# A written-out task order for block-sparse attention followed by a max-out layer: one order replaced by another

## The chip, the core and the metric
The kernel runs on one core of one Trainium2 chip. The metric is the device time of one execution in microseconds (us); lower is better. The kernel before was run 11 times: median 173.11 us, lowest 172.62, highest 173.88.

## The reference, cut to what matters
Two layers. The first is attention with a local window and block summaries, for 4 batches, 8 heads, 768 positions and 64 channels. The second is a layer that takes the larger of two products and multiplies it by a third matrix.

```python
k_sum = k.reshape(B, H, nb, 32, D).max(axis=3)      # one summary key per 32 positions
v_sum = v.reshape(B, H, nb, 32, D).mean(axis=3)
scores_l = where(|i - j| < 16, scale * q @ k.T, -1e9)
scores_s = scale * q @ k_sum.T + log(32)
a = softmax(concat([scores_l, scores_s]))           # max, exp, sum, divide
x = a @ concat([v, v_sum])                          # then [B, H, S, D] -> [3072, 512]
out = maximum(x @ w1, x @ w2) @ w_out               # 512 -> 1024 -> 512, float32
```

## The kernel before, in words
**The work is cut into 679 tasks.** Each call of `op` (line 111) adds a task: an engine, or several that could do it, a function that emits its instructions, and the buffers that it reads and writes. Tasks are numbered in the order of these calls. Nothing is emitted until `Plan.run` (line 128) walks a string, `ORDER` (line 20). A word of it such as `P455:2` says: emit task 455 now, on engine P, and let the new buffer that it writes take slot 2 of its ring. P is TensorE (PE), A is ScalarE (ACT), D is VectorE (DVE), G is GpSimd (POOL), S is SyncE (SP), whose tasks are DMAs. So the string fixes three things: the order on each engine's queue, the engine of each task that has a choice, and the buffer slot. Each engine works through its own queue strictly in order, and semaphores hold it until the data of a task are there.

**The tasks**, with their numbers, as far as they are spoken of below. "b" is the batch, "hp" a pair of heads (0 to 3), "grp" one of three groups of 256 positions.

- *load k, load q* (line 298): 384 KB each from HBM to one of eight `land` slots; one pair per b and hp. For b = 0: k00 is 12, q00 13, k01 36, q01 37, k02 38, q02 39, k03 40, q03 41 (batch, then hp). k10 is 146, q10 147. *load v* (line 320): two of 768 KB per batch (14 and 16 for b = 0, 178 and 180 for b = 2).
- *cast k, cast q* to bf16, *turn* (transposes on PE, line 434), *place* (copy from PSUM), and for k also *max*, *wrap*, *sums* (summary keys): lines 425 to 467. turn k10 is 220 and turn q10 221; turn k22 is 323, its load 174, its cast 321.
- *scores* (line 469), *exp* on ACT (line 515), *mask* on DVE (line 509), *values* (PE, line 543), *inv* and *x* on DVE (lines 549 and 552), *turn x* (PE, line 575) and *xt* (its copy). xt 00 is made by tasks 120 and 125.
- *cast v, spread v, means* (PE, lines 346 and 349), *spread means*: v and its block means laid out in `vx` (lines 320 to 396). cast v21 is 181, means 20 is 188, spread means 1 is 169, spread means 2 is 193.
- *load w* (line 594): w1 and w2 in two halves, 1 MB each: 42 and 43 (first halves), 52 and 53 (second halves). From each half come two *wd* = w2 - w1 (44, 48, 54, 58) and two *w1b* (a bf16 copy of w1: 45, 49, 55, 59), then *turn w1* (PE, line 618: 46, 50, 56, 60) and *w1t* (its copy from PSUM: 47, 51, 57, 61).
- *load wo* (line 627): w_out in two halves of 1 MB (62 and 65), each cast into two *wo* (63, 64 and 66, 67).
- *w1o* (line 636) = w1 @ w_out, in four column blocks, each with two PE tasks of four 128x512 matmuls that add up in one PSUM bank: 446/447, 449/450, 452/453, 455/456 for blocks 0 to 3. The first of a pair needs w1t 0, 1 and wo 0, 1; the second w1t 2, 3 and wo 2, 3, and so the second halves of w1 and w_out. The copies of the results are 448, 451, 454, 457.
- *hidden* (line 660): eight 128x256 matmuls each, four tasks per b and grp, each with its own wd. 458, 460, 462, 464 are 000, 001, 002, 003 (b, grp, and which wd). *relu* is its copy from PSUM. *out* (lines 674 and 681): three tasks of four 128x512 matmuls for 128 rows, first x @ w1o, then twice relu @ wo; *copy out* and *store* follow.

max(x w1, x w2) w_out is computed as relu(x (w2 - w1)) w_out + x (w1 w_out), which is why w1o is needed.

**PE works in four array shapes**, as the operands have them: 128*128 (hidden, out, w1o, means of b = 0), 64 rows (turn, scores), 128*64 (values), 128*32 (means of later batches). A stretch in one shape is followed by a stretch in another, some 70 times in the kernel.

In the order before, SP loads k03, k01, k00, q02, q00, q01, k02, q03, v00, v01, w 42, w 43, wo 62, w 52, wo 65, w 53, and then batch 1 in the order q10, k10, q13, k12, k13, q11, q12, k11, v11, v10.

Of the kernel before, what the change touches and what calls it, by code (L numbers as in the profile page):

```python
# [17 lines left out]


ORDER = (  # L20
    "G5:0 D6:0 D1 D2 D0 S40:0,0 S36:1,0 S12:2,0 S39:3,0 G23:0,0,0 G4:0 S13:0 S37:0 A101:0 S38:0 G7 "
    "G32:0,0 P103:0,0 G8 S41:0 A105:1,0 G68:1 A77:2 S14:4 D106:0 G9 P70:2,0 G93:3 P79:4,0 S16:5 A72:2,0 "
    "D81:0,0 G10 P95:6,0 A69:0 S42:6 D108 D82:1 A78:1 P71:0 S43:7 D73:0 A76:0 P80:0 D3 D92:2 A85:1 D102:3 "
    "P94:0 A100:2 D83 P104:0 D107 D75 D84 A96:3,0 D74 S62:2 P90:2 D97:0 P86:4 A91:0 D15:0,0 A109:3 D98 "
    "P24:6 D18 D99 D19 P114:2 S52:1 A25 D21 A87:1 P88:0 D20 G22 P110:6 A89:2 P112:4 D17:0 S65:3 D26 A28 "
    "P33:0 D29 D27 A34 A113:3 D30 P116:0 D35 S53:0 A31 P126:4 A111:4 G45:0 D117:0 D127:1 D118:0,0 A49:1 "
    "D128:0 G48:0 P121:6 P46:0 D122:2 S147:4,0 D123:1,0 P50:4 A47:1,0 D51:0 P119:6 A120:0 P124:0 P136:4 "
    "D125 G63:0 A115:5 P131:6 P460:0 S146:0 D44:0 A64:0 D137:0 A461:0 P458:1 D138:0 G55:0 P455:2 A459 "
    "S153:5,0 D59:1 P56:3 P60:0 D57:0 P452:5 A61:0 D132:1 D67:0 P449:3 A66:0 D11:0 S150:2,0 D133:0 P446:4 "
    "P450 S152:0 P453 D58:0 S149:6,0 P456 A219:0 D54:0 S151:0 P447 A457:0 D218:1 S148:0 P129:0 P134:6 "  # L30
    "P462:2 G163:1,0,0,0 D130:1 A135 D454:0 S156:7 A448:0 P464:0 D463 A258:2 S154:3 P141:6 P221:4,0 "
    "A451:0 P220:0 P480:1 D257:3 A465 S171:0,0 D142:2 A222:0,0 P478:2 G231:0 D481:1 S173:1,0 P476:3 "
    "D226:0 A479 G246:1 P471:0 D223:1 P260:1,0 D224 P139:4 P259:0 D245:2 P472 A140:2 D143:0 G230:3 "
    "A261:2,0 S170:0 P482:4 D225 D265:1 A477 P484:5 A483 D262:0 P144:6 G157:0,0 P227:1 P247:3,0 A145 "
    "P248:0 P485 D249:1,0 A228:1 P232:6,0 S175:4,0 D263 P233:0 P473 A234:3,0 D229 S172:0 A253:2 P500:1 "
    "D251 D264 D236 D235:1 G155:0 A474:0 P486 A501:2 P496:2 A487:1 D237 S162 D238:3 G295:2 P164:3 S161 "
    "P494:4 G307:1 A165 D250:0 A168 A497 P489:0 G294:3 D166 A495 D167 P242:5 D158 S169 P239:1 P266:3 "
    "A243:2 P498:7 D159 A267:4 P490 D252 D244 P502:5 A499 D160 S178:5 A240:0 S180:2 P269:3 P254:6 D268 "
    "S174:0 P503 S196:6,0 D306:0 A270:3 P491 D241 A255:5 G187:0,0,0,0 P284:1 D271 P504 D285:0 A492:2 "
    "D286:2,0 P507:3 A505:3 S493 D256 P275:6 P272:0 P278:4 D276:1 P508 D273:2 G179:0,0 D279:0 D274:0,0 "  # L40
    "P466:2 D280:0 S177:7,0 D277:0 P287:0 P281:4 P467 D282:2 S195:3,0 D288:0 D283:0 P509 G181:0 D289:0 "
    "S199:0,0 P296:6,0 P297:0 D510:4 P290:4 S176:0 A298:0,0 P292:0 G322:3 D291:3 P468 A302:0 S186 G321:2 "
    "D293 P188:3 P308:4,0 G183 S198:0 P309:0 P324:6,0 A310:3,0 P323:0 D314:3 P518:0 S185 A329:1 D311:1 "
    "P514:1 A519:1 S182 P536:4 A469:5 S200:1,0 G382:0 A515 P512:5 S197:0 A325:2,0 P520:0 G333:1 A190 "
    "S194:0 D326:0 A189 P516:2 G334:3 A513 D313 P335:6,0 P336:0 D517 P530:1 A337:1,0 D537:2 A341:2 P521 "
    "D328 S184 D312 D327 D299:1 A371:2 P315:4 P330:6 P534:2 S201:0 A316:4 D339 D338:0 P522 S506 D192 D535 "
    "P532:4 A523:2 S470 D531 A331:0 P552:5 D300 D340 D301 P525:2 G383:1 D553:0 P303:0 D191 G370:3 P345:6 "
    "S193 P526 A304:1 D317 S202:5 P543:5 S204:2 G211:1,0,0,0 D533 A346:2 S475 D332 P318:0 P342:3 P544 "
    "A319:3 D305 P527 A343:5 D320 S488 P545 D528:3 P548:6 D546:5 P550:7 D344 A549 P357:0 A551 P354:3 S529 "
    "P351:5 D358:1 P538:2 D352:2 D355:0 D353:1,0 P554:7 D356:0 P561:5 D359:0,0 A555 P360:3 D347 P384:6,0 "  # L50
    "S524 P373:0,0 D361:2 G410:0 P372:0 P385:0 D362:0 P562 A374:2,0 S547 G409:2 D390:1 A378:0 P556:3 "
    "G205:0,0 D386:0,0 P563 P348:0 A564:0 G203:0 P363:6 P539 D349:0 D364:1 S565 D365:0 P557 D350:0 S207 "
    "G209 P412:4,0 S208 P411:0 P368:6 P366:0 S206 A369:0 P558 S511 D367 P540 G210 D387:0 A417:3 P586:0 "
    "D375:1 A398:3 P572:1 A587:1 D376 D397:1 P590:6 A559:1 D541:3 A413:3,0 P602:7 D377 D591 P212:0 A603:0 "
    "P584:3 D214 A215 D414:1 A573:2 P568:2 A585 D388 D416 P604:4 D389 A213 A216 S217 P570:5 A605 A569 "
    "P379:6 D571 P399:0,0 P391:3 A380:0 P400:0 P579:2 D401:1,0 A392:3 P588:5 D403 D381 P566:6 D402:1 A589 "
    "P597:7 A567 D405:2 P592:3 D415 D404 P574:4 P394:5 P421:0 P580 A395:4 P593 A422:5 P575 D423 P406:5 "
    "P418:0 D396 P581 A407:1 D393 P594 A582:2 D408 A419:2 P608:5 P576 A609 D420 A595:5 P598 A577:0 S596 "
    "P439:0 P433:5 S560 P424:2 D440:2 P599 D434:1 S578 D425:0 D426:2,0 P606:4 A600:4 D441:0,0 P615:2 "
    "D435:0 S601 A607 P436:0 P427:5 P430:3 D437:0 P610:7 D438:0 D431:2 P616 D428:1 D432:0 P611 D429:0 "  # L60
    "P444:0 P442:3 A445:3 P617 D443 P612 A618:5 P674:5 P624:6 P644:3 D625:2 P658:4 P620:0 P628:1 A621 "
    "A659:1 P656:2 P642:6 D657 P622:0 D613:1 D645:0 P626:4 S614 A623 D643 S583 P640:2 A627 P638:7 P629 "
    "D639 P669:3 D641 P664:0 P633:6 P660:4 P634 D661 P662:7 P630 D663 P651:2 A631:0 P635 P646:4 D636:4 "
    "P665 S637 S542 P647 S619 P652 S632 P648 P666 A649:1 P653 S650 A667:2 P675 S668 D654:4 P670 P676 S655 "
    "P671 A677:3 A672:5 S678 S673 "
)


# [713 lines left out]
```

## Time and profile before

| | us |
|---|---|
| median of 11 runs | 173.11 |
| the profiled execution, its own time | 173.14 |
| its span, first to last instruction | 171.4 |
| outside the span (173.14 - 171.4) | 1.74 |
| PE busy, all of the span | 150.6 |
| DVE / ACT / POOL busy | 105.8 / 91.6 / 41.8 |
| PE idle to 34.5 us (34.51 less the 17.97 busy between 4.8 and 34.6, and 0.07 counted before) | 16.5 |
| after the last matmul | 3.1 |
| mean granted PE clock | 0.989 |

How to read it: the busy shares alone say that PE is the fullest engine. They don't say when. PE's idle time lies almost wholly in the first fifth of the span, where the inputs are still on their way; from there on it is busy without a gap but for one. The time is a sum of three parts with different limits: the start, the full part, the tail.

### The profile page before, as it was taken

To read this page: it belongs to the slowest core of one execution; us is meant where nothing else is said; L and a number is where in the kernel's file an instruction comes from. 1 tells how busy PE (TensorE), PEld (TensorE's weight loads), DVE (VectorE), ACT (ScalarE), POOL (GpSimd) and SP (SyncE) were. 2 spreads that over 40 slices of the span, in tenths; PEclk is the share of its full clock that TensorE was granted. 3 is DMA by queue.
4 is the path that set the end of the run, shared out by engine and by line. 5 is a ranking of instruction groups with operands and counts; after the bars stand their busy time and mean duration, and the time that the engine had idled before them with its cause. 6 is when DMAs were issued, how large, how long until landed. Compare 5 with 4: busy or idle time off the path is not lost.

```text
span 171.4 us, 5208 instructions
## 1 busy us (share of the span) xinstructions
PE 150.6 (88%) x2256; PEld 98.1 (57%) x2256; DVE 105.8 (62%) x198; ACT 91.6 (53%) x128; POOL 41.8 (24%) x62
## 2 busy tenths in 40 slices
PE   0155946799999999997999999999999999999992
PEld 0144636545856655475765764787555658876451
DVE  1276999558788998865778696674643761442110
ACT  3487498646658695067658433778368231320121
POOL 7720125600355401297121029400000000000000
PEclk9999997899999999999999999999999999999999
DMA  5999799999999779999995995764000600030175
GB/s 179 298 343 219 192 398 388 385 378 373 296 221 302 234 147 226 303 386 253 259 252 116 239 280 208 171 146 81 10 0 9 240 4 0 4 122 0 47 259 184
DMA packets 43430, 34.92 MB, mean 204 GB/s; under 512 B 25968, under 2 KB 37392, under 8 KB 43408
## 3 DMA queue, kind: packets, MB, share of 16 engines
q1 hardware_dynamic: 43408, 34.61, 73.0%
q8 instruction: 17, 0.28, 0.7%
q14 instruction: 5, 0.04, 0.1%
HBM read 25.17 MB, written 6.29 MB: 184 GB/s over the span
## 4 chain that ended last, share of the span: by engine, by line
PE 78%; DMA 14%; SPq 2%; issue 1%; POOL 1%; ACT 1%; DVE 1%; POOLq 0%; ACTq 0%
PE banks L681 25%; PE banks L660 24%; PE banks L674 12%; DMA land<-in_moe_w_dram 8%; DMA land<-in_v_dram 6%; PE banks L644 4%; PE banks L543 3%; PE banks L501 3%; PE banks L434 3%; SPq L305 2%; PE banks L575 2%; POOL w1b L410 1%; PE banks L349 1%; PE banks L346 1%; DVE vb L410 1%
## 5 line engine op out<-in xcount | busy, mean ns | idle before, releaser
L660 PE MATMUL banks<-xt,wd 128*128 128x256 bf16 x384 | 46.5, 274 | 1.0 <-issue 1.0
L681 PE MATMUL banks<-wo,g 128*128 128x512 bf16 (+1 forms) x200 | 46.4, 371 | 0.0
L660 PEld LDWEIGHTS <-wd 128*128 128x128 bf16 x384 | 37.0, 98 | 9.1 <-issue 1.2
L515 ACT ACTIVATE pb<-banks,bias 128x1024 bf16<-128x1024 f32 x24 | 26.1, 1114 | 6.4 <-PE banks L501 6.3
L681 PEld LDWEIGHTS <-g 128*128 128x128 bf16 x200 | 18.2, 98 | 17.2
L406 ACT ACTIVATE g<-banks 128x512 bf16<-128x512 f32 x30 | 17.6, 601 | 16.2 <-PE banks L660 16.2
L674 PE MATMUL banks<-w1o,xt 128*128 128x512 bf16 (+1 forms) x100 | 24.2, 371 | 0.0
L408 DVE TENSOR_SCALAR g<-banks 128x512 bf16<-128x512 f32 x18 | 12.1, 688 | 18.2 <-PE banks L660 17.4
L410 POOL CAST kqb<-land 128x768 bf16<-128x768 f32 x17 | 14.1, 836 | 29.6 <-DMA land<-in_q_dram 14.5
L410 ACT COPY o<-banks 128x512 f32<-128x512 f32 (+1 forms) x18 | 10.1, 565 | 20.4 <-PE banks L681 20.2
L434 PE MATMUL banks<-identity,kqb 64*128 64x64 bf16 x384 | 10.0, 202 | 10.2 <-ACT kqb L410 6.0
L454 DVE TENSOR_REDUCE ks<-kx 128x24 bf16<-128x768 bf16 x16 | 15.0, 945 | 6.4 <-ACT kx L410 6.4
L410 ACT COPY kx<-banks 128x768 bf16<-128x768 bf16 x12 | 9.7, 805 | 12.9 <-PE banks L434 12.9
L509 DVE TENSOR_TENSOR pb<-pb,mask 128x1024 bf16<-128x1024 bf16 x18 | 12.3, 704 | 6.3 <-ACT pb L515 6.2
L552 DVE TENSOR_TENSOR xs<-banks,inv 128x512 bf16<-128x512 f32 x24 | 15.6, 684 | 0.3
L434 PEld LDWEIGHTS <-kqb 64*128 64x128 bf16 x384 | 7.6, 102 | 13.2 <-ACT kqb L410 6.3
L674 PEld LDWEIGHTS <-xt 128*128 128x128 bf16 x100 | 9.5, 98 | 8.7
L410 POOL CAST vb<-land 128x1536 bf16<-128x1536 f32 x6 | 8.9, 1494 | 15.2 <-DMA land<-in_v_dram 15.2
L543 PEld LDWEIGHTS <-pb 128*64 128x64 bf16 x384 | 7.7, 114 | 6.8 <-issue 5.5
L543 PE MATMUL banks<-vx,pb 128*64 128x65 bf16 x384 | 9.0, 200 | 2.9 <-ACT pb L515 1.8
L501 PEld LDWEIGHTS <-kx 64*128 64x128 bf16 x416 | 8.1, 100 | 4.4 <-issue 3.7
L410 ACT COPY xt<-banks 128x512 bf16<-128x512 bf16 (+1 forms) x6 | 5.2, 870 | 10.1 <-PE banks L575 10.1
(66 smaller groups left out, 144.2 us busy)
## 6 DMA issues: line engine op xcount, KB each, us to landing
land<-in_k_dram SPq DMA_DIRECT2D x16, 384.0 KB, 8.1
land<-in_q_dram SPq DMA_DIRECT2D x16, 384.0 KB, 7.3
land<-in_v_dram SPq DMA_DIRECT2D x8, 768.0 KB, 10.9
out_dram<-o SPq DMA_DIRECT2D x19, 256.0 KB, 2.6
land<-in_moe_w_dram SPq DMA_DIRECT2D x4, 1024.0 KB, 11.3
land<-in_moe_w_out_dram SPq DMA_DIRECT2D x2, 1024.0 KB, 12.9
vx<-vb SPq DMA_DIRECT2D x3, 396.0 KB, 6.5
vx<-vx SPq DMA_DIRECT2D x3, 363.0 KB, 4.2
```

Source lines behind the costliest of these rows:

```text
L406: nc.scalar.activation(out=o, in_=i, func=ACT.Relu)
L410: {"DVE": nc.vector.tensor_copy, "ACT": nc.scalar.copy, "POOL": nc.gpsimd.tensor_copy, "SP": nc.sync.dma_start}[e](out=o, in_=i)
L434: nc.tensor.transpose(out=bank(ps, 2048, BF16)[:, at:at + 64], in_=src.ap[r, j].rearrange("p h d -> p (h d)"), identity=identity[r, r])
L454: op("DVE", 0.95, lambda: nc.vector.tensor_reduce(out=ks.ap[:].rearrange("p (t s) -> p t s", s=2), in_=kt()[:, :, 0:64].rearrange("p t (s ...
L501: nc.tensor.matmul(**m)
L509: nc.vector.tensor_tensor(out=o, in0=o, in1=m, op=ALU.mult)
L515: op("ACT", 1.13, lambda: nc.scalar.activation(out=pb.ap[:].rearrange("p a n -> p (a n)"), in_=bank(ps, 1024), func=ACT.Exp, bias=bias[:], ...
L543: nc.tensor.matmul(out=av()[64 * par:64 * par + 64, c, 2 * u + a, :], lhsT=pb.ap[:, a, at:at + 64], rhs=vx[b].ap[:, 4 * grp + 2 * u + par, ...
L552: op("DVE", 0.69, lambda: nc.vector.tensor_tensor(out=x.ap[:, grp] if g1 == grp else x.ap[:, grp:g1 + 1, hp % 2], in0=av()[:, :, :, 0:D], ...
L660: nc.tensor.matmul(out=bank(ps)[:, 256 * s:256 * s + 256], lhsT=wd[n].ap[:, c, 128 * s:128 * s + 128], rhs=x_rows(b, grp)[:, c, :], start= ...
L674: nc.tensor.matmul(out=bank(ps, hi - lo), lhsT=x_rows(b, grp)[:, c, sl], rhs=w1o[c].ap[:, lo:hi], start=(c == 0), stop=False)
L681: nc.tensor.matmul(out=bank(ps, hi - lo), lhsT=g.ap[:, f, sl], rhs=wo[f // 2].ap[:, f % 2, lo:hi], start=False, stop=(f == FC - 1))
```

## The change
Only `ORDER` is replaced. The 679 tasks are the same, so are their instructions but for the engine that some run on: 77 tasks change their engine (29 from DVE to ACT, 27 from ACT to DVE, 6 from DVE to POOL, 5 from ACT to POOL, 3 from POOL to DVE, 2 from POOL to ACT, 2 from SP to DVE, 2 from POOL to SP, 1 from SP to POOL). PE and the loads keep theirs. Many tasks take another slot. The order differs on all engines.

The beginning (to the first tasks of batch 2) and the end of the diff; what lies between is of the same kind:

```diff
 ORDER = (
-    "G5:0 D6:0 D1 D2 D0 S40:0,0 S36:1,0 S12:2,0 S39:3,0 G23:0,0,0 G4:0 S13:0 S37:0 A101:0 S38:0 G7 "
-    "G32:0,0 P103:0,0 G8 S41:0 A105:1,0 G68:1 A77:2 S14:4 D106:0 G9 P70:2,0 G93:3 P79:4,0 S16:5 A72:2,0 "
-    "D81:0,0 G10 P95:6,0 A69:0 S42:6 D108 D82:1 A78:1 P71:0 S43:7 D73:0 A76:0 P80:0 D3 D92:2 A85:1 D102:3 "
-    "P94:0 A100:2 D83 P104:0 D107 D75 D84 A96:3,0 D74 S62:2 P90:2 D97:0 P86:4 A91:0 D15:0,0 A109:3 D98 "
-    "P24:6 D18 D99 D19 P114:2 S52:1 A25 D21 A87:1 P88:0 D20 G22 P110:6 A89:2 P112:4 D17:0 S65:3 D26 A28 "
-    "P33:0 D29 D27 A34 A113:3 D30 P116:0 D35 S53:0 A31 P126:4 A111:4 G45:0 D117:0 D127:1 D118:0,0 A49:1 "
-    "D128:0 G48:0 P121:6 P46:0 D122:2 S147:4,0 D123:1,0 P50:4 A47:1,0 D51:0 P119:6 A120:0 P124:0 P136:4 "
-    "D125 G63:0 A115:5 P131:6 P460:0 S146:0 D44:0 A64:0 D137:0 A461:0 P458:1 D138:0 G55:0 P455:2 A459 "
-    "S153:5,0 D59:1 P56:3 P60:0 D57:0 P452:5 A61:0 D132:1 D67:0 P449:3 A66:0 D11:0 S150:2,0 D133:0 P446:4 "
-    "P450 S152:0 P453 D58:0 S149:6,0 P456 A219:0 D54:0 S151:0 P447 A457:0 D218:1 S148:0 P129:0 P134:6 "
-    "P462:2 G163:1,0,0,0 D130:1 A135 D454:0 S156:7 A448:0 P464:0 D463 A258:2 S154:3 P141:6 P221:4,0 "
...
+    "D1 G5:0 D2 D0 D3 S36:0,0 S12:1,0 S37:0 S40:2,0 G4:0 S38:3,0 S39:0 S13:0 G77:0 S41:0 D68:1 D11:0 "
+    "P70:0,0 A78:2 D6:0 G32:0,0,0 S14:4 P79:2,0 D72:1,0 G7 A81:2,0 P80:0 S16:5 D101:3 A85:0 D73:0 G92:1 "
+    "P103:4,0 S42:6 A105:0,0 D82:1 P94:6,0 G93:0 S43:7 A96:3,0 D75 P95:0 D84 G69:2 D106:0 G8 D97:1 A102:3 "
+    "P71:0 G9 A76:1 D74 D98 D83 D107 S62:0 D108 A100:2 D99 P86:2 G10 P88:0 A87:0 P90:6 D15:0,0 P104:0 "
+    "A89:1 D109:3 G22:0 P24:2 G23:0 A21 D18 P110:0 S52:3 D19 A25 D20 A91:2 D17:0 S65:1 D26 A28 P33:3 D30 "
+    "P112:4 D29 A34 P126:6 D27 A111:3 D35 P116:2 S53:2 A49:0 G31 D117:0 D127:1 G45:1 D118:0,0 P121:0 "
+    "A113:4 D128:0 P50:2 G48:0 D122:2 P46:6 S147:4,0 D51:1,0 P119:4 A47:0 D123:1,0 P114:2 D120:0 P124:0 "
+    "P131:6 A115:5 D125 P136:4 D44:0 P460:0 A64:0 S152:5,0 D63:0 P458:1 D137:0 D132:1 D133:0 A55:0 G59:1 "
+    "P452:2 D138:0 S146:0 P455:3 A459:0 D461 P60:6 P56:4 P449:1 D57:0 A66:0 G67:0 D61:0 P446:0 S153:0 "
+    "P134:4 P129:6 P456 A130:1 S151:6,0 A135 P450 D58:0 S150:0 P447 A219:1 D54:0 S154:7 P453 A448:0 "
+    "P464:6 S148:0,0 A451:0 G163:1,0,0,0 D454:0 P462:7 D218:0 S149:0 D465 P141:4 A463 G258:2 P221:0,0 "
...
+    "A165 D236 D251 A166 D168 G307:0 A501 P266:0 D167 P242:2 S169 P239:5 A267:0 D252 P498:4 D160 A243:3 "
...
+    "G294:1 D282:1 P467 D289:0 A510:4 D283:0 P290:3 G181:0 S511 P296:5,0 P297:0 D291:3 S200:0,0 A322:1 "
+    "P292:1 P468 S176:0 G321:3 A298:1,0 D293 S184:0,0,0 P188:7 G187:0 A469:5 P309:3,0 D302:0 P308:0 "
...
-    "P671 A677:3 A672:5 S678 S673 "
...
+    "P671 A677:1 A672:5 S678 S673 "
 )
```

In words, what the steps below use:

- The loads of batch 0 come as k01, k00, q01, k03, k02, q02, q00, q03; v and the weights follow in the same order as before. Batch 1 comes as q10, k13, k10, q13, q12, k12, v10, k11, q11, v11.
- PE around the second half of the weights, before: hidden 001, hidden 000, w1o 3 (first), turn w1 2, turn w1 3, w1o 2, 1, 0 (first), w1o 1, 2, 3, 0 (second), turn x010, turn x011, hidden 002, hidden 003, values 0 22 32, turn q10. After: hidden 001, hidden 000, w1o 2, w1o 3 (first), turn w1 3, turn w1 2, w1o 1, w1o 0 (first), turn x011, turn x010, w1o 3, 1, 0, 2 (second), hidden 003, hidden 002, values 0 22 32, turn q10.
- w1b 2 goes from POOL to ACT, w1b 3 from DVE to POOL; wo 0 from POOL to DVE, wo 3 from DVE to POOL; xt 000 from ACT to DVE; spread means 2 and one spread of v1 from SP to DVE; spread v21 from POOL to SP, spread v31 from SP to POOL.
- The tail: the last five PE tasks and the last two copies and stores are the same.

## The prediction
> **What bounds the kernel now.** I read the page's chain of work first, then busy time by window, then the chain in order of time, then PE's own waits.
>
> The chain by engine, from the page:
>
> ```profile
> PE 78%; DMA 14%; SPq 2%; issue 1%; POOL 1%; ACT 1%; DVE 1%; POOLq 0%; ACTq 0%
> ```
>
> PE carries the chain, with DMA behind it. Where each of them does so is in the windows (columns: stretch, length, then busy us and count for PE, weight loads, DVE, ACT and POOL, then granted PE clock, DMA share, GB/s):
>
> ```profile
> 4.80:34.60 29.80, 17.97 (x382) 13.09 (x384) 21.48 (x39) 21.46 (x27) 11.13 (x17) 0.94 1.04 319
> 34.60:168.30 133.70, 132.66 (x1880) 85.01 (x1878) 83.65 (x153) 67.71 (x99) 27.24 (x27) 1.00 0.68 180
> 168.30:171.40 3.10, 0.00 (x0) 0.00 (x0) 0.00 (x0) 0.37 (x1) 0.00 (x0) 0.93 0.43 152
> ```
>
> Up to 34.6 us PE is busy 18 us and the DMA engines all the time (share 1.04, 319 GB/s). From 34.6 to 168.3 PE is busy 132.66 of 133.70 us: only 1.04 us is lost. So an order can win time in three ways: let PE do more before 34.6, make its work after that shorter, or remove the 1.04. The tail has the same tasks in both orders.
>
> The chain in order of time shows where the first part ends (start, length, what):
>
> ```profile
> 19.89 12.94 DMA land<-in_moe_w_dram
> ...
> 32.98 1.48 POOL w1b L410
> 34.46 0.05 issue
> 34.51 0.64 PE banks L618 x32
> 35.15 6.15 PE banks L644 x28
> 41.30 0.34 PE banks L575 x16
> 41.64 1.85 PE banks L660 x16
> 43.49 0.37 PE banks L543 x16
> 43.87 0.46 PE banks L434 x24
> ...
> 54.39 0.87 PE banks L660 x8
> 55.27 0.86 PE banks L681 x4
> 56.13 0.87 PE banks L660 x8
> 57.00 0.45 PE banks L346 x24
> 57.45 0.98 PE banks L660 x8
> ...
> 78.24 1.04 issue
> ```
>
> The second half of w1 (load 52) lands at 32.84; POOL casts it in 1.48; turn w1 (L618) starts at 34.51; then nothing stops until the 1.04 at 78.24. The reader should also see that the same task costs 0.87 behind another of its shape (54.39) and 0.98 behind means, another shape (57.45): **a change of array shape costs 0.11**.
>
> PE's waits say the same of what preceded 34.51 (total, times, longest):
>
> ```profile
> PE banks L618 <- POOL w1b L410: 1.2, 1, 1.2
> PE banks L660 <- issue: 1.0, 1, 1.0
> ```
>
> **The change, part by part.**
>
> *The loads.* Before turn w1 the DMA queue holds the same 16 transfers, and the last eight stand in the same order in both. In the trace they land one after another: the eight k and q about 1.05 us apart up to 12.79, v00 at 16.38, v01 20.45, the weights at 23.35, 27.41, 30.11, 32.84, 35.56 and 38.29 (landing times of SP's issues). The DMA engines are full (share 1.04), so another order of the first eight moves none of the later landings. The slots that the new order gives them (wo 62 into 0, w 52 into 3, wo 65 into 1, w 53 into 2) were filled by k and q of batch 0, whose casts are over by about 13.7 (q03 lands 12.79 plus ACT's cast at 0.83), before SP gets there at 19.4. Price: 0.
>
> *The restart of PE at 34.51.* Two things must be ready: a w1b, and PE itself.
> w1b 3 on POOL: load 52 at 32.84, start 32.98. Its price is 1.04 (POOL's cast at 23.47, nothing of its kind on DVE beside it) or 1.47 (the cast at 32.98, beside DVE's cast 32.86 to 33.55). The new order takes that DVE cast away (w1b 2 goes to ACT), so I take 1.04: ready at 34.05, at worst 34.5.
> PE: hidden 000 needs wd 0. On DVE xt 000 now stands ahead of it: 0.42 (the xt row at 29.19). xt 001 ended at 29.61, so now about 30.0, and wd 0 (1.38) at 31.4; then hidden 000, half of the 2.34 that two took at 30.12: 32.5; then two w1o tasks at 0.86 to 1.03 each (PE row at 32.30): 34.2 to 34.5. wo 0 (0.64 on DVE after wd 0: 32.0) and wo 1 (ACT, 1.05 from 30.2) are there in time.
> I take 34.3: **-0.2**, ends 0 and -0.45.
>
> *One w1o task more before the restart.* Before, one of the eight w1o tasks ran ahead of turn w1; now two do. The time after the restart is shorter by one task of four 128x512 matmuls: **-0.86** (row 55.27, the same form; the seven of L644 took 6.15, 0.88 each). This is the main term. It holds if nothing between turn w1 and turn q10 makes PE wait. I went through it with rows of the trace, counting from 34.3: two turn w1 (0.64) and w1o 1, 0 (1.73) to 36.7; two turn x (0.34) to 37.0; then w1o second halves, which need wo 3. That is now POOL's, from 35.56 (landing of load 65), 1.04 to 1.64 (the two POOL rows of that size, 23.47 and 30.17): 36.6 to 37.2, a wait of 0 to 0.2. Four w1o halves end at 40.5. wd 3 is ready at 38.3 + 1.2 = 39.5 and wd 2 at 40.7 (DVE's pair at 38.32 took 2.36), for hidden 003 and 002 at 40.5 and 41.4. Cast k10 (load 146, now third of its batch, lands a transfer later, 41.4; DVE 0.55 after the copy of w1o 2) is ready at 42.0; its turn comes at 42.8. Nothing there is late.
>
> *Array shapes.* Counted in both orders from the first turn w1 to the end: before 60 changes, after 58. 2 x 0.11: **-0.2**, ends 0 and -0.2.
>
> *Later tasks.* PE reaches everything about 1.2 earlier, so whatever used to be just in time may be late.
> The tightest is batch 2. In the trace v21 lands at 72.47, POOL casts it 72.59 to 74.06, PE takes means 20 (L346) at 74.73. With PE 1.1 to 1.2 ahead it asks at 73.6: a wait of 0.45, if v21 lands as before. But spread means 1, which SP issues ahead of v20 and v21, waited until 59.73 for two copies of means on DVE, which stood behind a 0.94 max; now no max stands there, and one spread less is in the DMA queue. So v21 may come a microsecond earlier and the wait be 0.
> I also compared, for every PE task from turn q10 on, the PE work that lies between it and the task whose result it waits for. The least reserve after the copy or relu in between is about 0.5 before and 0.6 now: no general tightening.
> The engine moves of the later part: spread means 2 on DVE has no row; DVE's 32x2904 copy at 0.97, twice, gives 1.9, and values of batch 2 come at 97, far behind. DVE has 83.65 busy in 133.70, so this room hides it; without it each would cost its own length.
> For both tight places (wo 3 0 to 0.2, means 20 0 to 0.45) I take **+0.15**, ends 0 and 0.65.
>
> *The 1.04 at 78.24.* It is called "issue": no semaphore is waited for. In the trace the record of the instruction queue (17 packets, 0.28 MB on the page) has a packet at 76.67 that took 1.1, and PE goes on at 79.28. I infer that PE ran out of instructions after the dense stretch of transposes (144 small matmuls, each with its weight load, between 72.6 and 76.0). The new order has the same stretch in front of the same place in the instruction stream, about 1.1 earlier: I take the same stall, **0**; ends -1.04 (gone) and +1.04 (twice as long, or one more of its size).
> The Trainium skill (Runtime: NRT & Kernel Launch, section "Instruction fetch mechanics") says that a crossing to the next 16 KiB of instructions is mostly hidden; by this the term would be -1.04 and not 0, but this trace shows one crossing that wasn't.
> The same skill (SBUF — State Buffer, section "The single rule") has DVE and GpSimd excluding each other on a shared port for a whole instruction; POOL's cast would then have been 1.04 + 0.57 = 1.61 beside the DVE cast, where the trace has 1.47, and without it 1.04 as taken above.
>
> **The sum.** -0.2 - 0.86 - 0.2 + 0.15 + 0 = -1.1. The profiled execution took 173.14 (span 171.4 plus 1.74), close to the median 173.11: 173.14 - 1.1 = **172.0**.
>
> **The rivals.**
> 1. *The gain is larger.* The fetch at 76.7 falls into a gap of the data transfers and the 1.04 goes: 173.14 - 1.1 - 1.04 = 171.0. For: the stall exists only because one packet came late. Against: the DMA queue is as full there in both.
> 2. *The gain is eaten by late data.* Restart unchanged at 34.5, shapes worth nothing, both tight places at their ends: -0.86 + 0.65 = -0.2: 172.9. For: the DMA engines set v21's landing, and they don't get faster. This is also how the change would fail to do what it says.
> 3. *Slower: the instruction queue.* PE asks for instructions 1.1 earlier while the DMA engines are as full as before. The trace's loads wait between 3.2 and 15.3 in that queue, so a packet of instructions can well come 2 later. It decides from where the stall grows by more than 1.1 (from 1.04 to over 2.2, or a second one opens ahead of it). Twice the present stall and one more of its size, 2.08 more: 173.14 - 1.1 + 2.1 = 174.1. Against: 16 of 17 such packets cost nothing in this trace.
>
> **How the numbers follow.** Forecast 0.52 (171.5 to 172.5, by the ends of the terms without the stall); rival 1: 0.12; rival 2: 0.16; rival 3: 0.20. 0.2% of 173.11 is 0.35, about what a measurement of this kernel can tell from no change. The forecast and rival 1 lie under 172.76: faster 0.64; rival 2 lies within: 0.16; slower 0.20. The range goes from rival 1 (171.0 less 0.1) past rival 2 and half a microsecond of growth of the stall: 170.9 to 173.6; it leaves out most of rival 3.
>
> **What would show it.** L618 starting within 34.0 to 34.5; two groups of four L644 ahead of it; turn q10 (L434 x24 after L543) at 42.5 to 43.0 in place of 43.87; PE's wait list with no line but a small one after 35; the "issue" gap of some 1.0 near 77. The prediction is wrong if L618 starts after 34.8, if an "issue" gap longer than 2 appears, or if means 20 or a turn of batch 2 waits for a load.

## The result and the profile after

The kernel after took 171.51 us in the median of 13 runs (169.97 to 173.0); the kernel before, run beside it, 173.16. The ratio (after over before) is 0.987, 95% interval 0.9848 to 0.9893: faster, by 1.65 us in the medians. The profiled execution of after took 171.13 (span 169.4), that of before 173.14 (span 171.4): 2.0 less. The forecast was 172.0, a gain of 1.1.

The ratios, here and below, leave out every execution that lies more than 1.5% above the fastest of its kernel (4 of the 13 of after, with clocks like those of the others, and 9 of 12 in one experiment), while the medians hold all of them and give 0.990 here.

The chain of work by engine, from the page of after:

```profile
PE 78%; DMA 8%; DVE 7%; SPq 3%; issue 2%; ACT 1%; ACTq 0%
```

PE carries as much of the chain as before. The DMA share is down from 14% to 8%, and DVE has come in with 7%: two things that the prediction had not expected. The same two windows as in the prediction (columns as there):

```profile
4.80:34.60 29.80, 20.16 (x413) 14.70 (x414) 24.01 (x45) 21.59 (x24) 12.93 (x21) 0.89 1.12 344
34.60:168.30 133.70, 131.40 (x1844) 84.35 (x1843) 82.83 (x144) 67.41 (x103) 27.60 (x30) 1.00 0.66 175
```

To 34.6 us PE has 31 matmul records more (413 against 382), at a clock of 0.89 in place of 0.94, and the DMA engines move 344 GB/s in place of 319. The chain of after in order of time, around the restart:

```profile
5.65 13.34 DMA land<-in_v_dram
...
29.37 2.89 PE banks L660 x16
32.26 1.73 PE banks L644 x8
33.99 0.57 PE banks L618 x32
34.56 1.83 PE banks L644 x8
...
42.04 0.38 PE banks L543 x16
42.41 0.46 PE banks L434 x24
```

Two groups of four L644 now stand ahead of L618, as predicted. But the chain does not come to L618 from the load of the weights and its cast: it runs back through PE to the load of v. The timeline of after says why (start, length, operation, idle time before it):

```profile
30.93 1.04 ACT L410 CAST w1b<-land 128x1024 bf16<-128x1024 f32 x1 [0.72 <-DMA land<-in_moe_w_dram]
31.00 1.04 POOL L410 CAST w1b<-land 128x1024 bf16<-128x1024 f32 x1 [3.26 <-DMA land<-in_moe_w_dram]
```

The weights landed at 30.85 (load 52; 32.84 before) and both w1b were ready at 32.04. PE was busy until 33.92. Two lines from the list of PE's waits in after (total, times, longest); the only one of that list that lies behind 34 us is the second:

```profile
PE banks L618 <- DVE xs L552: 0.4, 1, 0.4
PE banks L501 <- DVE vx L410: 0.2, 1, 0.2
```

(The L618 of the first line is turn w1 of the first half of the weights, at 25.67.) The "issue" gap of 1.04 is not there any more.

**Where the 2 us are**, from PE's records in the two profiled executions (second turn w1 is the first L618 behind 30 us):

| | before | after | difference |
|---|---|---|---|
| second turn w1 starts | 34.51 | 33.92 | -0.59 |
| from there to turn q10 | 9.29 | 8.43 | -0.86 |
| from turn q10 to PE's end | 124.50 | 123.89 | -0.61 |
| PE's end | 168.30 | 166.24 | -2.06 |

The last stretch holds -1.04 (the gap gone) and +0.25 (a wait at 58.90, the second line of the waits); 0.18 goes the other way and is not explained.

### The profile page after: what moved, and what is told of

Same layout as the page of the kernel before. It is cut to its first block, busy times and chain, and to the rows that moved or that the text cites. A ratio compares the mean times of both kernels' runs of the same rounds, so it can differ in the third digit from the quotient of the medians.

```text
span 169.4 us, 5194 instructions
## 1 busy us (share of the span) xinstructions
PE 151.6 (89%) x2256; PEld 99.1 (58%) x2256; DVE 107.2 (63%) x195; ACT 90.3 (53%) x127; POOL 44.0 (26%) x67
## 4 chain that ended last, share of the span: by engine, by line
PE 78%; DMA 8%; DVE 7%; SPq 3%; issue 2%; ACT 1%; ACTq 0%
PE banks L660 24%; PE banks L681 24%; PE banks L674 12%; DMA land<-in_v_dram 8%; PE banks L644 4%; PE banks L543 4%; PE banks L501 4%; DVE vx L410 3%; PE banks L434 3%; SPq L305 2%; PE banks L575 2%; DVE ks L454 1%; PE banks L618 1%; DVE kx L461 1%; DVE kx L410 1%
## 5 line engine op out<-in xcount | busy, mean ns | idle before, releaser
L681 PE MATMUL banks<-wo,g 128*128 128x512 bf16 (+1 forms) x200 | 45.7, 371 | 0.0
L660 PEld LDWEIGHTS <-wd 128*128 128x128 bf16 x384 | 37.5, 99 | 8.3
L406 ACT ACTIVATE g<-banks 128x512 bf16<-128x512 f32 x34 | 19.2, 598 | 21.9 <-PE banks L660 21.9
L410 POOL CAST kqb<-land 128x768 bf16<-128x768 f32 x22 | 18.7, 857 | 32.1 <-DMA land<-in_q_dram 24.1
L408 DVE TENSOR_SCALAR g<-banks 128x512 bf16<-128x512 f32 x14 | 9.6, 688 | 19.4 <-PE banks L660 19.4
L509 DVE TENSOR_TENSOR pb<-pb,mask 128x1024 bf16<-128x1024 bf16 x18 | 11.7, 683 | 3.2 <-ACT pb L515 3.2
L501 PE MATMUL banks<-qx,kx 64*128 64x64 bf16 (+2 forms) x416 | 9.7, 195 | 1.1 <-ACT qx L410 0.9
L410 ACT COPY qx<-banks 128x768 bf16<-128x768 bf16 x10 | 7.9, 799 | 4.4 <-DVE kx L410 3.3
```

The costliest lines, as they stand in the source:

```text
L406: nc.scalar.activation(out=o, in_=i, func=ACT.Relu)
L410: {"DVE": nc.vector.tensor_copy, "ACT": nc.scalar.copy, "POOL": nc.gpsimd.tensor_copy, "SP": nc.sync.dma_start}[e](out=o, in_=i)
L501: nc.tensor.matmul(**m)
L509: nc.vector.tensor_tensor(out=o, in0=o, in1=m, op=ALU.mult)
L660: nc.tensor.matmul(out=bank(ps)[:, 256 * s:256 * s + 256], lhsT=wd[n].ap[:, c, 128 * s:128 * s + 128], rhs=x_rows(b, grp)[:, c, :], start= ...
L681: nc.tensor.matmul(out=bank(ps, hi - lo), lhsT=g.ap[:, f, sl], rhs=wo[f // 2].ap[:, f % 2, lo:hi], start=False, stop=(f == FC - 1))
```

## The experiments

**One more execution of each of the two kernels** (labels r_before and r_after), to see how much one execution says.

> The kernel before, once more, for a second trace. Theory 1 (the loads of the first 38 us always land as in the first trace, and the 1.04 us issue gap is a fixed part of the order): load 52 lands at 32.8 within 0.3, the issue gap is there with 1.0 within 0.3, near 78. Theory 2 (both differ from one execution to the next): load 52 lands up to 2 us earlier, or the gap is missing or of another length.

> The changed kernel, once more. Theory 1 (its earlier landings come from its order of loads): load 52 lands at 30.9 within 0.3 again, and there is no issue gap. Theory 2 (chance): load 52 lands anywhere from 30.5 to 33. The granted clock in the first 35 us: if the half-clock stretch of 6.8 us is chance, it has another length now (0, 3.4, 6.8 or 10.2), and the span moves with it.

Measured: 173.26 and 170.06. Second turn w1 at 34.79 and 32.24, turn q10 at 44.08 and 40.82, from there to PE's end 124.33 and 124.34. So in this pair the whole difference at PE's end, 3.25, lies ahead of turn q10. The before trace has no "issue" gap this time, only a wait of 0.42 at 82.82 for a cast on POOL. What repeats in both pairs is the start: load 52 lands at 32.84 and 33.1 before, at 30.85 and 31.0 after. What does not repeat is who comes last at turn w1. In the profiled after it was PE; in this trace PE waits for the cast:

```profile
32.24 0.64 PE L618 MATMUL banks<-identity,w1b 64*128 64x64 bf16 x32 [0.30 <-POOL w1b L410]
```

**Where the earlier landings come from.** The windows of single microseconds show it, first of before, then of after:

```profile
5.00:6.00 1.00, 0.44 (x12) 0.27 (x12) 0.00 (x0) 0.52 (x1) 0.94 (x5) 1.00 0.86 221
18.00:19.00 1.00, 1.00 (x7) 0.43 (x6) 0.96 (x4) 0.09 (x1) 0.29 (x1) 1.00 0.42 70
19.00:20.00 1.00, 1.00 (x26) 0.71 (x24) 0.99 (x2) 0.97 (x2) 0.00 (x0) 1.00 0.25 51
```

```profile
5.00:6.00 1.00, 0.19 (x8) 0.19 (x10) 0.81 (x3) 0.00 (x0) 0.94 (x4) 1.00 1.07 378
18.00:19.00 1.00, 0.55 (x18) 0.41 (x19) 0.95 (x2) 0.94 (x2) 0.00 (x0) 1.00 1.02 331
19.00:20.00 1.00, 0.00 (x0) 0.00 (x0) 0.96 (x1) 0.54 (x1) 0.00 (x0) 1.00 1.04 389
```

The last two columns are the ones to read. Before, the transfers have two holes: 221 GB/s at 5 us, while k and q still come in, and 70 and 51 GB/s (DMA share 0.42 and 0.25) around 19 us, at the end of v. After, neither is there. In the first hole single packets of 1536 bytes, mostly 0.06 us each, take up to 1.0 us (1.4 in the second trace of before; 0.5 at most in the profiled after). The second hole lies where SP is still busy issuing the first halves of w1 and w2, to 19.25 before and to 16.97 after (start, length; before, then after):

```profile
13.67 5.58 SPq L599 DMA_DIRECT2D land<-in_moe_w_dram  x2
```

```profile
12.81 4.16 SPq L599 DMA_DIRECT2D land<-in_moe_w_dram  x2
```

What holds SP there is not shown. The average of the whole stretch, 319 GB/s at a share of 1.04, on which the prediction rested, hides both.

**The loads of after in the kernel before** (e_before_loads_of_after), and the other way round (e_after_loads_of_before). Only the eight words of the loads of batch 0 change places (the words between them left out):

```diff
-S40:0,0 S36:1,0 S12:2,0 S39:3,0 S13:0   S37:0 S38:0   S41:0
+S36:1,0 S12:2,0 S37:0   S40:0,0 S38:3,0 S39:0 S13:0   S41:0
```

```diff
-S36:0,0 S12:1,0 S37:0   S40:2,0 S38:3,0 S39:0 S13:0 S41:0
+S40:2,0 S36:0,0 S12:1,0 S39:3,0 S13:0   S37:0 S38:0 S41:0
```

> The kernel before, with the first eight loads (k and q of batch 0) issued in the changed kernel's order, all else as before. Theory 1 (the order of these loads makes the hole in the transfers at 4 to 7 us and the later hole at 18 to 20 us, and through them the landing of all weights): no holes, v01 lands at 18.9, load 52 at 31.0 in place of 32.8 to 33.1; the time falls by 1 to 1.8, ratio 0.990 to 0.995, less what the casts lose by waiting for other loads. Theory 2 (the holes come from what the engines do meanwhile): load 52 still lands at 32.8 or later, ratio 1.00 or above.

> The changed kernel, with the first eight loads in the order of the kernel before. Theory 1: the holes come back, load 52 lands at 32.8 to 33.1, turn w1 starts at 34 or later and the time rises by 1 to 2 over the changed kernel: ratio to the kernel before 0.993 to 1.0. Theory 2: load 52 lands at 31.0, the time rises by less than 0.7 (casts that wait for other loads), ratio 0.985 to 0.991.

Measured for the first: the holes are gone. Its windows:

```profile
5.00:6.00 1.00, 0.00 (x0) 0.00 (x0) 0.00 (x0) 0.00 (x0) 0.92 (x4) 1.00 1.04 383
18.00:19.00 1.00, 0.59 (x3) 0.43 (x4) 0.98 (x4) 0.20 (x1) 0.51 (x1) 1.00 1.05 311
19.00:20.00 1.00, 1.00 (x7) 0.44 (x6) 0.96 (x4) 0.09 (x1) 0.29 (x1) 1.00 1.04 383
```

Load 52 lands at 31.3, and yet the ratio is 1.0038 (0.9998 to 1.0078): no gain. A cast on ACT whose data now come later holds PE's first turns for 8.4 (4.9 before), and PE still waits 1.1, 0.69 and 1.1 between 24.9 and 27.6 for ACT's copies and exps: the same three waits as before, 1 us later. Turn q10 is at 43.57.

For the second the first hole is back (229 GB/s at 5 us), load 52 lands at 31.9, between the two expectations, turn q10 moves from 42.35 to 44.71, and the ratio is 1.002 (0.9974 to 1.0066), though it rests on three executions only; the median of all twelve is 175.48, which is 1.012 of the 173.4 of before beside it. Together: the order of the first loads does decide when everything behind them lands; it pays only with engine orders that use it.

**k03 put fourth instead of first** (e_before_k03_fourth), to find which load makes the holes.

```diff
-S40:0,0 S36:1,0 S12:2,0 S39:3,0 S13:0 S37:0 S38:0 S41:0
+S36:1,0 S12:2,0 S39:3,0 S40:0,0 S13:0 S37:0 S38:0 S41:0
```

> The kernel before with one load moved: k03 comes fourth (k01, k00, q02, k03, q00, q01, k02, q03) in place of first; all else as before. If it is k03 at the head of the queue (or three k in a row) that makes the two holes in the transfers, they are gone: over 350 GB/s from 4 to 7 us, 18 to 20 us over 300 GB/s, v01 landing at 19.0 and load 52 at 31 as with the whole new order of loads. If the holes come from another pair of neighbours among the first eight, one or both stay: under 300 GB/s at 5 us, v01 at 20 or later, load 52 at 32 to 33. For the time both expect no gain, a ratio of 0.998 to 1.008, since earlier weights alone gave none.

```profile
5.00:6.00 1.00, 0.00 (x0) 0.00 (x0) 0.00 (x0) 0.00 (x0) 0.92 (x4) 1.00 0.94 283
18.00:19.00 1.00, 0.12 (x6) 0.00 (x0) 1.00 (x2) 1.00 (x2) 0.00 (x0) 1.00 1.17 212
```

Half of each. 283 GB/s at 5 us with packets of up to 1.3 us, so k03 at the head is not, or not alone, what makes the first hole; the second is mostly closed, and load 52 lands at 31.4. The time missed both expectations: 1.0119 (1.0068 to 1.0171). The cast of k03 stands first on its engine and now waits for the fourth load (PE's longest wait for it 9.4, 4.9 before); turn q10 is at 46.1. What in the order makes packets slow stays open.

**The main term by itself.** In the kernel before, the second w1o task is moved ahead of turn w1 (e_before_two_ahead); in the kernel after, it is moved back behind it (e_after_one_ahead).

```diff
-D59:1 P56:3 P60:0 D57:0 P452:5 A61:0
+D59:1 P452:5 P56:3 P60:0 D57:0 A61:0
```

```diff
-P452:2 D138:0 S146:0 P455:3 A459:0 D461 P60:6 P56:4 P449:1
+P452:2 D138:0 S146:0 A459:0 D461 P60:6 P56:4 P455:3 P449:1
```

> The kernel before with one word moved: the first task of w1o 2 goes ahead of turn w1 2, as the change does. Theory of the prediction (turn w1 waits for the cast of w1b, and one more w1o task fits into that wait): faster by 0.86, ratio 0.995, and turn q10 starts some 0.9 earlier than in the kernel before. Rival (PE itself is late there, by the half clock): no change, ratio within 0.9985 to 1.0015.

> The changed kernel with one word moved: the first task of w1o 3 goes behind turn w1 2, so that one w1o task is ahead as in the kernel before. Theory of the prediction: slower than the changed kernel by up to 0.86. Rival (w1b is ready at 32.0, nearly 2 us before PE comes to turn w1, so nothing waits there): no change against the changed kernel, that is a ratio of about 0.987 to the kernel before.

Measured: 1.0011 (0.998 to 1.0043) for the one, 0.9886 (0.9839 to 0.9934) for the other. Adding the step gains nothing, taking it away loses nothing that can be measured; but the interval of the second, 0.5% to either side, is as wide as the 0.86 us that were in question, so it doesn't exclude them. In the trace of the first, turn w1 starts at 35.92 and turn q10 at 45.03: PE, not the weights, was late, so the task ahead only moved turn w1 back. It also made a wait of its own:

```profile
35.92 0.64 PE L618 MATMUL banks<-identity,w1b 64*128 64x64 bf16 x32
37.19 5.34 PE L644 MATMUL banks<-wo,vx 128*128 128x512 bf16 x23 [0.62 <-DVE vx L410]
```

The w1o task behind turn w1 (449) writes bank 3, which turn w1 2 (56) has just filled, and waits until DVE has copied it out (57, to 37.13). The task that was moved ahead had stood between them. In the kernel after, the two have different banks (`P56:4`, `P449:1`), so this experiment isn't a clean test of the step. In the second, PE waits 0.69 at turn w1, which starts at 32.24, and turn q10 is at 41.53, still earlier than in the profiled after:

```profile
32.24 0.64 PE L618 MATMUL banks<-identity,w1b 64*128 64x64 bf16 x32 [0.69 <-POOL w1b L410]
```

That wait is idle time in which the task, had it been left ahead, would have cost little.

**Half of the order each.** h_start_after has the new order up to turn q10 and the remaining tasks in the old order (7 buffers take other slots); h_start_before has the old order up to turn q10 and the rest as in the new.

```diff
-ORDER, all words of before
+words of after ahead of P221, then the words of before that are left
```

```diff
-ORDER, all words of before
+words of before ahead of P221, then the words of after that are left
```

> A hybrid: the changed kernel's order up to turn q10 (the start), then what is left in the order of the kernel before; seven buffers get another slot, because theirs are taken. Theory of the prediction, corrected (the start carries the gain, the rest only the 2 changes of array shape less and the chance of the issue gap): turn q10 at 40.8 to 42.4, from there to PE's end 124.3 to 125.5; ratio 0.985 to 0.992. Rival (half of the gain is the later part, where the kernel before stops 1 us): ratio 0.992 to 0.996.

> The old order up to turn q10, then the remaining tasks in the new order. Theory: most of the gain needs the new start, and the new later part gives some 0.3 to 0.5 us of its own (no issue gap, two changes of array shape fewer): turn q10 at 43.8 to 44.1, from turn q10 to the end of TensorE 123.9 to 124.4, ratio 0.995 to 1.0. Rival: the new later part alone carries the gain (the start is worth nothing by itself, as the start alone was worth only 0.2%): ratio 0.987 to 0.992, which would need 122.5 from turn q10 to the end.

| | ratio | turn q10 | from there to PE's end |
|---|---|---|---|
| before | 1 | 43.80 | 124.50 |
| new start, old rest | 0.9978 (0.9947 to 1.0009) | 41.91 | 125.96 |
| old start, new rest | 1.0097 (1.006 to 1.0134) | 44.71 | 126.18 |
| after | 0.987 (0.9848 to 0.9893) | 42.35 | 123.89 |

Neither half brings the gain, and both expectations were missed: the second was to be 0.995 to 1.0. The new start does put turn q10 1.9 earlier, but the old rest gives 1.5 of it back: 0.9 in two waits that before has not (0.68 at 59.35 for DVE, 0.22 at 50.41), and some 0.6 that is not explained; its issue gap of 0.98 stands in before too (1.04). The old start with the new rest shows waits at the seam, for casts on POOL; these stand behind a cast of v at 54.08, for whose load POOL had been idle 6.34:

```profile
56.38 0.35 PE L434 MATMUL banks<-identity,kqb 64*128 64x64 bf16 x12 [0.56 <-POOL kqb L410]
57.60 0.35 PE L434 MATMUL banks<-identity,kqb 64*128 64x64 bf16 x12 [0.87 <-POOL kqb L410]
```

So the two ratios don't say what a half is worth by itself; they say that neither half works as well with the other order's half as with its own.

**The clock.** In the profiled after PE ran at half its clock ahead of turn w1. Windows of after (granted clock third from the end):

```profile
24.00:26.00 2.00, 0.93 (x29) 0.88 (x30) 1.94 (x5) 0.99 (x1) 0.61 (x1) 0.66 1.05 385
26.00:28.00 2.00, 2.00 (x62) 1.62 (x58) 1.94 (x5) 1.01 (x1) 1.74 (x1) 0.50 1.05 387
28.00:30.00 2.00, 2.00 (x51) 1.65 (x46) 1.62 (x3) 1.84 (x2) 0.00 (x0) 0.50 1.06 388
30.00:32.00 2.00, 2.00 (x14) 1.51 (x13) 1.97 (x6) 1.25 (x2) 1.00 (x1) 0.63 1.05 386
```

The stretch is 6.83 us long, from 24.64, behind waits of PE of 1.5, 0.8 and 1.3 since 20.0; in the profiled before it is 3.41 long, from 27.6. In it two hidden tasks take 2.89 (the chain at 29.37) where two take 1.75 at the full clock (at 40.29), so PE loses over 1 us there, just ahead of turn w1. The runs of after point the same way: the seven with a mean granted clock of 0.99 or more have a median of 170.45 us, the six with 0.98 or less 172.1. That doesn't say which is the cause, since the waits of PE could bring both the half clock and the longer time. The Trainium skill (TensorE: Matmul & The Clock Gate, section "What's actually happening") has two states, half and full, and a free-running window of 3413 ns; the lengths here, 3.41 and twice that, agree.

To test whether this sets the time, e_after_warm adds 28 matmuls of 128x240 to the kernel after, whose results nothing uses:

```diff
+    def warm(n):
+        for _ in range(n):
+            nc.tensor.matmul(out=bank_tile[:, 2, 260:500], lhsT=identity[:],
+                             rhs=hide_t[:].rearrange("p w n -> p (w n)")[:, 0:240], start=True, stop=True)
-P110:0 S52:3
+P110:0 W10 S52:3
-P116:2 S53:2
+P116:2 W18 S53:2
```

> The changed kernel with 28 extra 128x240 matmuls on data that nobody reads, in two idle stretches of PE: 10 ahead of means 04 (idle 18.5 to 20.0), 18 ahead of values 0 20 30 (idle 22.3 to 24.6). Theory (the half-clock stretches of 3.4 or 6.8 us that begin near 24.6 come from PE's idle time before them, and cost the changed kernel what its runs differ by, 170.0 to 173.0): no half clock between 15 and 35, span 168.2 to 168.7, median 170.2, spread under 1. Rival (the spread comes from the loads or from instruction supply): the clock is full but the median stays at 171.3 and the spread at 2 or more. If the extra matmuls come late and hold up PE: slower than 171.5.

Measured: the clock is 1.0 throughout, and the ratio is 0.9894 (0.9853 to 0.9935), the median 171.36, the spread still 2.5. The half clock goes and the time stays. In this trace PE comes to turn w1 at 33.44, hardly earlier than 33.92, after waits of 1.26 and 0.72 at 23.56 and 26.92 for work on ACT and DVE. That the half clock costs after nothing is not shown by that, for the 28 matmuls take time of their own; that removing it in this way is no gain, is.

**A store.** The trace of that run showed PE waiting 1.70 at 104.3 for a copy on ACT that waited for a store to free its slot of `o`; in the profiled after the same copy waits 1.28, without harm to PE. e_after_store lets SP issue the store of block 010 (488) earlier and gives copy out 121 (564) the slot that this frees; e_after_store_warm adds the 28 matmuls.

```diff
-A316:1 S475 P520:3
+A316:1 S475 S488 P520:3
-P348:0 A564:5
+P348:0 A564:1
-D414:0 S560 S488 P579:6
+D414:0 S560 P579:6
```

> The kernel after with one store issued earlier (010, from behind store 120 to behind store 001 on SP) and copy out 121 put into the slot of the output ring that this frees, so that this copy on ScalarE no longer waits for a store of batch 1 at 103 us. Theory: that wait makes the after kernel's times differ by 3 us from execution to execution; without it the ratio to before is 0.982 to 0.986 and the runs lie within 1.5 us. Rival: the wait was hidden in most executions (TensorE waited 0 for it in the first trace), so the ratio stays at 0.986 to 0.990 and the spread at 2 to 3 us.

> The same with the 28 extra matmuls of the earlier run, which keep TensorE's clock up ahead of 32 us (their results are used nowhere). Theory: with neither the half clock nor the wait for the store left, the runs lie within 1.5 us and the ratio is 0.980 to 0.985. Rival: neither of the two sets the time; ratio 0.987 to 0.991 and a spread of 2 us or more, as with the extra matmuls alone.

The copy of after, and then the same copy in e_after_store, which waits for nothing any more:

```profile
102.64 0.59 ACT L410 COPY o<-banks 128x512 f32<-128x512 f32 x1 [1.28 <-DMA out_dram<-o]
```

```profile
101.04 0.59 ACT L410 COPY o<-banks 128x512 f32<-128x512 f32 x1
```

Measured: 0.9829 (0.9781 to 0.9877), runs from 169.51 to 171.68 but for one at 173.4, and 0.986 (0.9813 to 0.9906) with the extra matmuls. The first is the lowest ratio of the study, but its interval overlaps that of after, so whether the store helps is not settled; its runs still differ by 2 us and more, so the wait is not the cause of that. What does show in this trace is who takes an earlier start back:

```profile
58.05 0.21 PE L501 MATMUL banks<-qx,kx 64*128 64x48 bf16 x4 [0.65 <-DVE kx L458]
58.74 0.41 PE L501 MATMUL banks<-qx,kx 64*128 64x64 bf16 x16 [0.48 <-DVE vx L410]
```

Turn q10 is at 41.13 here, 1.2 earlier than in the profiled after (42.35). These scores start at 58.74 against 58.90, and from there PE needs 107.4 to its end, against 107.3.

## Why the prediction was right, and where it was not

The sign, the size and the range were right (forecast -1.1, measured -1.65 by medians and -2.0 by the profiled executions). The reasons hold only in part, and that the number came out is partly luck. In the profiled pair, -2.06 at PE's end, the restart gave -0.59 for the -0.2 of the forecast, the one w1o task -0.86 as forecast, shapes and tight places together +0.43 for -0.05, and the gap -1.04 for 0. In the other pair the restart gave -2.55, the stretch behind it -0.71, and everything behind turn q10 nothing.

- **The loads: the DMA engines are full, "so another order of the first eight moves none of the later landings", price 0.** Wrong, and the step from which the rest went astray. Load 52 lands 2 us earlier; with the eight loads exchanged alone, in either direction, the first hole comes or goes with them, and load 52 moves to 31.3 in the kernel before. The landings that the prediction read as about 1.05 us apart have one step of 2.44 among them (k01 at 5.05, k00 at 7.49): that is the first hole. The share of 1.04 is a mean over 30 us, and in the first hole the share is still 0.86 at 221 GB/s; the windows of one microsecond would have shown the holes beforehand. Alone, the earlier landings are worth nothing (1.0038); they pay with the new order of the engines.
- **The restart, -0.2 to 34.3.** Measured -0.59 (33.92) in one pair and -2.55 (32.24) in the other. The cast on POOL took 1.04, as taken. The prediction had its two conditions within half a microsecond of each other (w1b at 34.05, PE at 34.2 to 34.5). In the profiled after w1b was there at 32.04 and PE came 1.9 later; in the second trace of after PE came first and waited 0.30 for w1b. So the landing of the weights moved the restart in one, PE's own delay held it up in the other.
- **"One w1o task more before the restart: -0.86. This is the main term."** The stretch behind turn w1 is shorter by just that, 0.86. But the term counted the task as free ahead of turn w1, in PE's idle time there. That idle time is 1.18 in the profiled before and 0.36 in the second trace of before. In the profiled after, with the second task ahead, PE has none left: what was saved behind turn w1 was largely spent ahead of it. In the second trace of after 0.30 is left even so, and there the task was free. So the term holds where the weights come last and fails where PE does, and that differs from one execution to the next. The experiment on it in the old order found no gain, but made a wait of 0.62 of its own; the one in the new order is too coarse to find 0.86. What the step is worth in the median stays open.
- **Array shapes, -0.2.** Not seen and not isolated: behind turn q10, with the gap and the new wait taken off, after is 0.18 longer.
- **Tight places, +0.15.** wo 3 and means 20 made PE wait for nothing (v21 landed at 70.50, 2 us earlier than before). A place that the prediction had not named became tight instead: scores of batch 1 at 58 us, behind work on DVE (in one trace on ACT). In six traces with the new order they wait 0.25, 0.72, 0.48, 1.13, 1.15 and 0 where turn q10 is at 42.35, 40.82, 41.53, 41.13, 41.93 and 41.87.
- **The issue gap, 0.** It went, as in rival 1; five of six traces with the old rest of the order have it (0.84 to 1.07), and of the six with the whole new order and its loads none (nothing above 0.2). With a change to the start, the new rest of the order has smaller ones: 0.32 at 81.78 behind the old start, 0.48 at 104.55 behind the old loads. The instruction packet that came at 76.67 before comes at 73.19 in after. Rival 3, the same queue getting worse, did not occur.
- **Rival 2**, gain eaten by late data, has its share: 0.25 at 58.90 in the profiled after, up to 1.15 where the start is earlier still.

In sum, what the runs show is a gain of 1.5 to 3.3 us at turn q10 that needs both the earlier landings and the new order of the engines: either alone gave none (1.0038 and 1.002). Less of it is given back with the new rest of the order than with the old one. How much single moves of tasks add was not tried beyond the one w1o task. Why the old order of the first loads slows single packets stays open, as does the spread of after's runs (3.0 us in 13 runs; 1.9 in the 48 runs of before beside them, but for one).

## What to carry to other kernels

Before a load order is priced at nothing because the queue is "full", look at GB/s in windows of a microsecond: the two holes here (221 in place of 378 GB/s at 5 us, 51 in place of 389 at 19) went with landings of the weights up to 2 us later. Compare like with like, though: from 13 to 14 us, in the loads of v with their packets of 256 bytes, both orders move 217 GB/s, and that is no hole. A task put into an idle stretch is worth no more than the idle time that is there in every execution, so read that wait in more than one trace. A gain at the start is kept only if the later order asks for nothing sooner than the other engines can give it: swap halves of two orders to see whether they fit together.

## What the runs showed of the hardware that was not expected

- The order of eight loads of 384 KB, all in the same queue, changes the rate: 343 to 390 GB/s from 5 to 6 us with the new order (eight traces), 204 to 257 with the old one (five traces). The slowest packet of 1536 bytes between 4 and 8 us takes 0.24 to 0.87 us in the former and 1.02 to 1.46 in the latter; most take 0.06.
- With 28 matmuls that nothing needs, all twelve runs (e_after_warm and e_after_store_warm) had a mean granted clock of 0.997 or more, where the 13 runs of after had 0.97 to 1.0; the time did not change beyond its interval.
- The gap in which PE waits for no semaphore (0.84 to 1.07 us) is there in five traces with the old rest of the order, at 78 to 82 us, and not in a sixth, so one trace doesn't tell whether an order has it.
